# Holding the row scatters of an attention sequence until the twelfth exp of the next one

## The chip, the cores and the metric

The kernel runs on one core of one Trainium2 chip. The metric is the device time of one execution in microseconds (us). Three executions of the kernel before took 382.21, 382.22 and 384.64 us; the median is 382.22 us.

Engines are named as in the profile: PE (TensorE), with PEld for its weight loads, DVE (VectorE), ACT (ScalarE), POOL (GpSimd) and SP (SyncE, which here only issues DMAs).

## The reference

Attention with a learned bias over 8 sequences of 576 tokens and 8 heads of 64, and after it a mixture of 8 experts in which each token goes to the one expert that its domain id names.

```python
scores = (q @ k.T) / 8                               # per batch and head, 576 x 576
x = log1p(abs(i - j)) / log1p(max(i, 1))             # the same for all sequences
bias = relu(x[..., None] @ w1 + b1) @ w2             # hidden width 32, one value per head
attn = softmax(scores + bias)
rows = (attn @ v)                                    # back to 4608 rows of 512
for e in range(8):                                   # 1024 hidden
    mask = domain_id == e
    out[mask] = relu(rows[mask] @ moe_w1[e]) @ moe_w2[e]
```

## The kernel before

**Three stages.** First the bias tables are made, exp of the bias for all heads, kept in fast memory, and beside them the routing: for each token, the row of a scratch tensor `fire_x` in device memory to which it will go, so that the rows of an expert lie together (`posi`). Then attention runs over the sequences 0 to 7. Its results are scattered into `fire_x`, row by row, by indirect DMAs. Then the experts read `fire_x` back, transposed (`xT`, and `xA` for the first 512 rows of expert 0), multiply twice, and scatter the results into the output.

**Units of a sequence.** Each sequence has 21 units, numbered 0 to 20. A unit is a block of scores: PE multiplies (`scores`, lines 562 to 621), ACT takes the exp (line 614) of 128 x 1024 values, DVE multiplies by the bias table (`weight`, line 625). The order is: unit 0 `r0`, units 1 to 8 the main blocks of head pairs 0 and 1, unit 9 `r1`, units 10 to 13 head pair 2, units 14 and 15 `l0` and `l1` (last queries), unit 16 `x` (a quarter of the size, with a score buffer `scx` that it shares with the transposes), units 17 to 20 head pair 3. The scores of the others have two buffers, `sc`. The twelfth exp of a sequence is that of unit 11.

**The plan.** Behind each unit a written list, `PLAN`, says what else is done there. `T` and `D` transpose q and k of the next sequence on PE and copy them out on DVE; `V` copies v (`make_vext`); `W` weights a block; `A` multiplies by v into the accumulator `pu`, of which there is one (`av`, lines 630 to 658); `N` normalizes the result into a tile of rows (`norm`, lines 660 to 691). A mark ' says that it belongs to the sequence before. So the last four query blocks of head pair 3 of sequence b are finished at unit 7 of sequence b+1 (`N3'`), and its last 64 queries at unit 4 (`N4'`).

**Rows and scatters.** The rows of a sequence lie in two tiles: `xt` for 512 queries (four scatters of 128 rows of 1028 bytes, line 702) and `xl` for the last 64 (one scatter). Each has two buffers; a new one begins at `N0` (unit 11), where an iota on POOL writes the token numbers into its last columns (line 696). Half of `xl` is moved to its place by a copy that SP issues (line 691). In `norm`, as soon as head pair 3 is done, the four scatters of `xt` are issued, then a tiny memset of a tile `mark`, and then the scatter of `xl`. For sequence 7 the last norm is in two halves, each with its own two scatters.

**What sets the order.** PE, DVE and ACT execute in the order in which the code is written. POOL's queue is ordered by `_Issue` (lines 97 to 120): each DMA that POOL issues is kept behind the one that was written before it. The scatters of one group are free among each other, and whatever comes next stands behind all of them; this is what the memset of `mark` is for. Through POOL go, in a sequence b: the loads of q, k and their last rows for sequence b+2 (unit 2, lines 501 to 515), the scatters of sequence b-1 (unit 7), the load of v for b+2 with its last rows `vrag` (unit 8), the iotas (unit 11), and a load of a part of the experts' weights `w` (unit 12, line 983). In sequence 6 three more weight parts are loaded at unit 8 and one at unit 17. In sequence 7, SP issues the transposing read of `xA` at unit 9 (line 990). It has to wait for all scatters of sequences 0 to 6.

**Into the experts.** The first matmul of the experts (line 853) reads `xA`. The rest of expert 0 (line 861) reads `xT`, which waits for the scatters of sequence 7.

Of the kernel before, what the change touches and what calls it, by code (L numbers as in the profile page):

```python
# [13 lines left out]
AF = mybir.ActivationFunctionType  # L14
# [6 lines left out]
B = 8  # L21
# [71 lines left out]
def _ins(inst):  # L93
    return inst.ins if hasattr(inst, "ins") else inst
# [366 lines left out]
class _Attention:  # L461
# [100 lines left out]
    def scores(self, b, u):  # L562
        nc, G = self.nc, self.G
        mm = nc.tensor.matmul
        if u[0] == "x":
            sc = G.tps.tile([P, 1, 256], F32, tag="tr", name="scx", bufs=2)
        else:
            sc = G.aps.tile([P, 2, 512], F32, tag="sc", name="sc", bufs=2)

        j = self.joined.get(u)  # L570
        if j is None:
            e = self.new_e()
        else:
            if j == 0:
                self.e2 = self.new_e2()
            e = self.e2[:, 2 * j: 2 * j + 2, :]
        self.e[b, u] = e
        hs = (slice(0, 64), slice(64, 128))
        n = 1024
        if u[0] == "m":  # L580
            _, p, c = u
            raw = 2 * p >= RAW.get(c, H)
            if raw:
                for h2 in range(2):
                    mm(out=sc[:, h2, :], lhsT=G.idn, rhs=G.biasW[c][:, 2 * p + h2 - RAW[c], :],
                       start=True, stop=False)
            for h2 in range(2):
                mm(out=sc[:, h2, :], lhsT=self.qkT[b, p][hs[h2], 1, 128 * c: 128 * c + 128],  # L588
                   rhs=self.qkT[b, p][hs[h2], 0, :], start=not raw, stop=True)
            c0 = c if j is None else c - 1  # L590
            bias = None if raw else G.biasM[:, c0: c + 1, 2 * p: 2 * p + 2, :].rearrange("p c h i -> p c (h i)")
        elif u[0] == "r":
            for p in range(2):
                mm(out=sc[:, p, :], lhsT=self.qkTl[b][:, 2 * u[1] + p, 1, :],
                   rhs=self.qkT[b, 2 * u[1] + p][:, 0, :], start=True, stop=True)
            bias = G.biasR[:, 2 * u[1]: 2 * u[1] + 2, :].rearrange("p q i -> p (q i)")
        elif u[0] == "l":
            for lj in range(2):
                c = 2 * u[1] + lj
                for p in range(4):  # L600
                    mm(out=sc[:, lj, :].rearrange("k (h p q) -> k h p q", h=2, p=4)[:, :, p, :],
                       lhsT=self.qkT[b, p][:, 1, 128 * c: 128 * c + 128],
                       rhs=self.qkTl[b][:, p, 0, :].rearrange("k (h q) -> k h q", h=2),
                       start=True, stop=True)
            bias = G.biasL.rearrange("p u l h q i -> p (u l h q i)")
        else:
            n = 256
            for p in range(4):
                for h2 in range(2):
                    mm(out=sc[:, 0, 64 * p: 64 * p + 64], lhsT=self.qkTl[b][:, p, 1, :],  # L610
                       rhs=self.qkTl[b][:, p, 0, 64 * h2: 64 * h2 + 64], start=h2 == 0, stop=h2 == 1)
            bias = G.biasRL.rearrange("p q i -> p (q i)")
        ef, sf = e.rearrange("p a i -> p (a i)"), sc.rearrange("p a i -> p (a i)")
        nc.scalar.activation(out=ef[:, 0:n], in_=sf[:, 0:n], func=AF.Exp, bias=0.0, scale=0.125)  # L614
        if bias is None or j == 0:
            return None
        if j == 1:
            ef = self.e2.rearrange("p (c a) i -> p c (a i)", c=2) if u[0] == "m" else \
                self.e2.rearrange("p a i -> p (a i)")
            return ef, bias  # L620
        return (ef[:, 0:n].unsqueeze(1) if u[0] == "m" else ef[:, 0:n]), bias
# [38 lines left out]
    def norm(self, b, p, halves=(0, 1)):  # L660
        nc, asb = self.nc, self.G.asb
        pv = self.pu[:, :, 0:260].rearrange("p a (g d) -> p a g d", d=65)
        if p < 4:
            rz = asb.tile([P, 2, 4, 1], F32, tag="rz", name="rz", bufs=2)
            if p == 0:
                self.xt[b] = self.new_rows("xt", P, 4, S * b, 4)
                self.xl[b] = self.new_rows("xl", P, 1, S * b + 512, 1)
            a0, n = halves[0], len(halves)
            a = slice(a0, a0 + n)
            nc.vector.reciprocal(out=rz[:, a], in_=pv[:, a, :, 64:65])  # L670
            nc.vector.tensor_tensor(  # L671
                out=self.xt[b][:, 2 * a0: 2 * a0 + 2 * n, 128 * p: 128 * p + 128]
                .rearrange("p (a c) (g d) -> p a c g d", a=n, d=64),
                in0=pv[:, a, :, 0:64].rearrange("p a (c g) d -> p a c g d", g=2),
                in1=rz[:, a].rearrange("p a (c g) d -> p a c g d", g=2).to_broadcast([P, n, 2, 2, 64]),
                op=AO.mult)
            if p == 3:
                for t in range(2 * a0, 2 * a0 + 2 * n):
                    self.scatter(b, t, self.xt[b][:, t, :], 128)

                if b in self.xl:
                    self.G.issue(nc.gpsimd.memset(self.mark, 0.0))
                    self.scatter(b, 4, self.xl.pop(b)[0:64, 0, :], 64)
        else:
            rz = asb.tile([P, 2, 4, 1], F32, tag="rz", name="rz", bufs=2)
            xl = self.xl[b]
            pl = pv[:, 0]
            nc.vector.reciprocal(out=rz[:, 0], in_=pl[:, :, 64:65])
            nc.vector.tensor_tensor(out=xl[:, 0, 0:256].rearrange("p (g d) -> p g d", d=64), in0=pl[:, :, 0:64],
                                    in1=rz[:, 0].to_broadcast([P, 4, 64]), op=AO.mult)  # L690
            nc.sync.dma_start(out=xl[0:64, 0, 256:DM], in_=xl[64:128, 0, 0:256])

    def new_rows(self, tag, n, c, base, step):

        t = self.G.asb.tile([n, c, XW], F16, tag=tag, name=tag, bufs=2)
        self.G.issue(self.nc.gpsimd.iota(t[:, :, DM:].bitcast(I32), base=base, channel_multiplier=step,
                                         pattern=[[1, c], [0, 1]]))
        return t
# [19 lines left out]
    def run(self, late):  # L718
# [5 lines left out]
        for p in range(4):  # L724
            n = 4 if all(2 * p < RAW.get(c, H) for c in range(4)) else 2
# [23 lines left out]
        def plan(b, ui):  # L749

            if b < B - 1:
                return PLAN[ui].split()
            if b == B:
                return [w for w in PLAN[ui].split() if w[:2] not in ("A4", "N4")]
            return {19: "W16 N2 A40 A41", 20: "A42 A43 W18 N4"}.get(ui, PLAN[ui]).split()

        for n in range((B + 1) * NU):
            b, ui = divmod(n, NU)
            if b < B:
                jobs[b, ui] = self.scores(b, units[ui])  # L760
            if (b, ui) == (0, 5):
                self.nc.vector.memset(self.vx[1][:, :, :, 64:65], 1.0)
            if b == 0 and ui in (2, 6):
                self.transposes(0, 2 + ui // 6)
            if b == 0 and ui in (3, 7):
                self.take(0, 2 + ui // 7)
            if b < B - 2 and ui == 2:
                self.load_qk(b + 2)
                self.load_last(b + 2)
            if b < B - 2 and ui == 8:  # L770
                self.load_v(b + 2)
                self.load_vrag(b + 2)
            late(b, ui)
            for what in plan(b, ui):
                act(what.rstrip("'"), b - what.count("'"), n)
# [153 lines left out]
def kernel(  # L929
# [13 lines left out]
    nc = tc.nc  # L943
# [11 lines left out]
    with tc.manual_schedule(engines={ET.PE, ET.DVE, ET.Activation}):  # L955
        with ExitStack() as att:
# [20 lines left out]
            with tc.tile_pool(name="aps", bufs=1, space=PS, reuse_waits="tile") as G.aps:  # L977
                def late(b, ui):
                    if (b, ui) == (0, 2):
                        G.w.load(2, G.w_first)  # L980
                        _clear_overflow(tc, G, x_dram)
                    if 0 < b < 7 and ui == 12:
                        G.w.load(1, G.w_first)
                    if (b, ui) == (6, 8):
                        G.w.load(3, G.n4)
                    if (b, ui) == (6, 17):
                        G.w.load(1, G.n4)
                    if (b, ui) == (B - 1, 9):
                        G.early = G.n4("xA").rearrange("p (c t) -> p c t", c=4)
                        nc.sync.dma_start_transpose(out=G.early, in_=x_dram[0: EARLY, 0:DM])  # L990
                at.run(late)
# [36 lines left out]
```

## Time and profile before

| | us |
|---|---|
| median of three executions | 382.22 |
| the profiled execution | 384.64 |
| its span in the profile | 383.04 |
| PE busy | 330.2 (86%) |
| ACT busy | 250.6 (65%) |
| DVE busy | 237.0 (62%) |
| POOL busy | 180.4 (47%) |
| exps (line 614), busy and idle before them | 150.6 and 18.1 |
| scatters of `xt` (line 702), busy, mean of one | 40.2, 1.255 |
| attention's first exp of sequence 1, about | 88.8 |
| first matmul of the experts | 234.01 |

A time line of the profile gives the start in us from the start of the span, the length in us, the engine, the line of the kernel, the operation, what it writes and reads with the shapes, how many such instructions were merged into the row (x20), and in brackets the idle time of the engine just before the row and what ended it. The exps overlap a little: one takes 1.02 to 1.13 us, and the next starts about 0.90 us after it. The busy shares above are means over stages with different limits: in the stage of sequences 1 to 6 ACT and DVE are both busy nearly all the time, in the experts' stage PE alone is.

The ends of matmuls are modelled, and a small part of PE's records is missing in the trace.

### The profile page before, as it was taken

How to read it: one execution, taken by the hardware profiler on the slowest of the kernel's cores; microseconds unless marked ns; L12 is line 12 of the kernel's file. 1: busy time of each engine (PE TensorE's matmuls, PEld its weight loads, DVE VectorE, ACT ScalarE, POOL GpSimd, SP SyncE). 2: the span in 40 equal slices, each digit the busy share in tenths (PEclk: the TensorE clock that was granted, in tenths of full speed). 3: DMA queues.
4: the chain of work that ended last, by engine and by line, in shares of the span. 5: the costliest groups of instructions: out<-in, count | busy, mean ns of one | idle time of the engine just before them, and what ended most of it. 6: DMA issues, size and time to landing. Idle time of an engine off the chain costs nothing. (4 is left out here: it accounts for less than half of the span.)

```text
span 383.0 us, 9754 instructions
## 1 busy us (share of the span) xinstructions
PE 330.2 (86%) x4098; PEld 215.4 (56%) x4098; DVE 237.0 (62%) x450; ACT 250.6 (65%) x306; POOL 180.4 (47%) x236
## 2 busy tenths in 40 slices
PE   1488696959899898999898878999999999999990
PEld 0378673735657575656565554564646565565640
DVE  6999998739899999999999864212030302112130
ACT  8999996749799999999999963331505142332500
POOL 9260001883856859494546334234453635233241
PEclk9999999978999999999999989999999999999997
DMA  5999974939297999989727941699999999821221
GB/s 88 183 157 346 282 127 55 156 45 170 69 177 107 141 170 124 183 127 180 116 61 122 216 96 40 147 240 203 207 195 241 218 222 212 211 94 55 79 82 44
DMA packets 87668, 57.37 MB, mean 150 GB/s; under 512 B 44741, under 2 KB 78789, under 8 KB 87624
## 3 DMA queue, kind: packets, MB, share of 16 engines
q0 software_dynamic: 56960, 45.13, 69.5%
q1 hardware_dynamic: 30664, 11.62, 15.1%
q8 instruction: 32, 0.52, 0.6%
q14 instruction: 12, 0.10, 0.1%
HBM read 61.93 MB, written 24.70 MB: 226 GB/s over the span
## 5 line engine op out<-in xcount | busy, mean ns | idle before, releaser
L614 ACT ACTIVATE e<-sc 128x1024 f16<-128x1024 f32 x160 | 150.6, 1058 | 18.1 <-PE sc L588 11.0
L822 DVE COPY res<-ops 128x512 f32<-128x512 f32 x40 | 27.7, 692 | 109.4 <-PE ops L819 105.5
L879 ACT ACTIVATE hT<-hps 128x640 f16<-128x640 f32 x56 | 39.4, 704 | 78.1 <-PE hps L843 67.6
L625 DVE TENSOR_TENSOR e<-e,biasM 128x2048 f16<-128x2048 f16 x64 | 73.1, 1154 | 4.4 <-ACT e L614 4.1
L823 POOL DMA_INDIRECT out_dram<-res,ids x40 | 39.5, 987 | 74.2 <-DVE res L822 65.9
L819 PE MATMUL ops<-w,hT 128*128 128x512 f16 x320 | 70.7, 379 | 0.0
L702 POOL DMA_INDIRECT fire_x<-xt,posi x32 | 40.2, 1255 | 61.1 <-issue 45.6
L588 PE MATMUL sc<-qkT 64*128 64x512 f16 x256 | 53.1, 404 | 10.9 <-ACT e L614 7.9
L843 PE MATMUL hps<-xT,w 128*128 128x320 f16 x448 | 62.0, 299 | 0.0
L843 PEld LDWEIGHTS <-w 128*128 128x128 f16 x448 | 43.8, 98 | 18.1
L642 PE MATMUL pu<-vext,e 128*128 128x65 f16 x1024 | 51.6, 198 | 0.8 <-issue 0.4
L819 PEld LDWEIGHTS <-hT 128*128 128x128 f16 x320 | 31.2, 98 | 36.7 <-ACT hT L855 0.5
L642 PEld LDWEIGHTS <-e 128*128 128x128 f16 x1024 | 45.6, 101 | 3.1 <-issue 1.9
L787 POOL DMA_DIRECT2D w<-in_moe_w_dram x32 | 25.2, 792 | 18.7 <-DMA w<-in_moe_w_dram 7.1
L240 PE MATMUL eb<-W2BIG,e 128*128 128x32 f16 x432 | 19.6, 194 | 16.0 <-DVE e L223 9.6
L638 PE MATMUL pu<-vrag,e 128*128 128x130 f16 x128 | 29.6, 231 | 2.6 <-DVE xt L671 1.3
L588 PEld LDWEIGHTS <-qkT 64*128 64x128 f16 x256 | 16.6, 94 | 26.8 <-issue 17.3
L223 DVE TENSOR_SCALAR e<-L,slope,nb 128x576 f16<-128x576 f16 x86 | 31.1, 433 | 0.0
L240 PEld LDWEIGHTS <-e 128*128 128x128 f16 x432 | 17.5, 117 | 18.1 <-DVE e L223 10.9
L560 DVE COPY qkT<-pt 128x1024 f16<-128x1024 f16 x32 | 21.9, 685 | 5.3 <-PE sc L588 4.7
L671 DVE TENSOR_TENSOR xt<-pu,rz 128x512 f16<-128x512 f32 (+1 forms) x33 | 22.3, 675 | 1.8 <-DMA fire_x<-xt,posi 0.4
L638 PEld LDWEIGHTS <-e 128*128 128x128 f16 x128 | 12.7, 100 | 17.9 <-issue 11.3
(145 smaller groups left out, 394.0 us busy)
## 6 DMA issues: line engine op xcount, KB each, us to landing
w<-in_moe_w_dram POOLq DMA_DIRECT2D x32, 512.0 KB
fire_x<-zero SPq DMA_DIRECT2D x1, 5140.0 KB
qn<-in_q_dram POOLq DMA_DIRECT2D x8, 512.0 KB
kn<-in_k_dram POOLq DMA_DIRECT2D x8, 512.0 KB
vst<-in_v_dram POOLq DMA_DIRECT2D x8, 512.0 KB
out_dram<-res,ids POOLq DMA_INDIRECT x40
last<-zero SPq DMA_DIRECT2D x2, 256.0 KB
last<-in_q_dram POOLq DMA_DIRECT2D x16, 32.0 KB
```

The source lines that it names most:

```text
L223: nc.vector.tensor_scalar(out=hr, in0=G.L4[:, c0: c0 + S], scalar1=G.slope[:, m: m + 1], scalar2=G.nb1[:], op0=AO.mult, op1=AO.max)
L240: nc.tensor.matmul(out=eb[:, lj, 32 * k16: 32 * k16 + 32], lhsT=hr[:, jc: jc + 4 * 127 + 1: 4], rhs=G.W2BIG[:, 0:32], start=True, stop=True)
L588: mm(out=sc[:, h2, :], lhsT=self.qkT[b, p][hs[h2], 1, 128 * c: 128 * c + 128], rhs=self.qkT[b, p][hs[h2], 0, :], start=not raw, stop=True)
L614: nc.scalar.activation(out=ef[:, 0:n], in_=sf[:, 0:n], func=AF.Exp, bias=0.0, scale=0.125)
L625: self.nc.vector.tensor_tensor(out=job[0], in0=job[0], in1=job[1], op=AO.mult)
L638: mm(out=self.pu[:, c // 2, o: o + 130], lhsT=er[:, p % 2, 128 * c: 128 * c + 128], rhs=vr[:, p, :], start=True, stop=False, skip_group_ch ...
L642: mm(out=self.pu[:, c // 2, o + 65 * h2: o + 65 * h2 + 65], lhsT=self.e[b, ("m", p, j)][:, h2, 128 * c: 128 * c + 128], rhs=vx[:, 2 * p + ...
L702: inst = self.nc.gpsimd.indirect_dma_start(out=self.x_dram[:, :], out_offset=bass.IndirectOffsetOnAxis(ap=self.G.posi[0:n, c:c + 1], axis= ...
L819: nc.tensor.matmul(out=ops_, lhsT=hT[:, fc, t0: t0 + 128], rhs=G.w.w2(e, fc), start=(fc == 0), stop=(fc == 7))
L823: inst = nc.gpsimd.indirect_dma_start(out=out[:], out_offset=bass.IndirectOffsetOnAxis(ap=idx.bitcast(I32), axis=0), in_=res[:], in_offset ...
L843: nc.tensor.matmul(out=hps[:, i, 0:HC], lhsT=G.w.w1(e, dc)[:, 128 * fc: 128 * fc + 128], rhs=xT[:, dc, HC * hf: HC * hf + HC], start=(dc = ...
L879: nc.scalar.activation(out=hT[:, fc, :].rearrange("p (a b) -> p a b", a=2), in_=first(e, xT, ((fc, 0), (fc, 1))), func=AF.Relu, bias=0.0, ...
```

## The change

The scatters leave `norm`. `norm` now only notes that sequence b is ready (`self.ready`), but for the halves of sequence 7, which are scattered at once as before. The run loop issues the scatters of the ready sequence at unit 11 of the next one, and each of the four scatters of `xt` is made to wait for the exp of that unit. The memset of `mark` and the scatter of `xl` follow as before. The load of v and `vrag` moves from unit 8 to 12, the weight loads from 12 to 13 and (three in sequence 6) from 8 to 12, and the read of `xA` in sequence 7 from unit 9 to 12.

```diff
-        nc.scalar.activation(out=ef[:, 0:n], in_=sf[:, 0:n], func=AF.Exp, bias=0.0, scale=0.125)
+        self.exp = _ins(nc.scalar.activation(out=ef[:, 0:n], in_=sf[:, 0:n], func=AF.Exp, bias=0.0, scale=0.125))
...
             if p == 3:
-                for t in range(2 * a0, 2 * a0 + 2 * n):
-                    self.scatter(b, t, self.xt[b][:, t, :], 128)
-
-                if b in self.xl:
-                    self.G.issue(nc.gpsimd.memset(self.mark, 0.0))
-                    self.scatter(b, 4, self.xl.pop(b)[0:64, 0, :], 64)
+                if n == 1:
+                    self.scatters(b, (2 * a0, 2 * a0 + 1))
+                else:
+                    self.ready = b
...
+    def scatters(self, b, ts, behind=None):
+        for t in ts:
+            inst = self.scatter(b, t, self.xt[b][:, t, :], 128)
+            if behind is not None:
+                self.tc.add_manual_dep(_ins(inst), behind.name, mybir.DependencyInfo(
+                    mybir.DependencyClass.Sync, mybir.DependencyReason.DATA), reason="behind an exp")
+
+        if b in self.xl:
+            self.G.issue(self.nc.gpsimd.memset(self.mark, 0.0))
+            self.scatter(b, 4, self.xl.pop(b)[0:64, 0, :], 64)
...
                 jobs[b, ui] = self.scores(b, units[ui])
+            if 0 < b < B and ui == 11:
+
+                self.scatters(self.ready, range(4), self.exp)
...
-            if b < B - 2 and ui == 8:
+            if b < B - 2 and ui == 12:
                 self.load_v(b + 2)
                 self.load_vrag(b + 2)
...
-                    if 0 < b < 7 and ui == 12:
+                    if 0 < b < 7 and ui == 13:
                         G.w.load(1, G.w_first)
-                    if (b, ui) == (6, 8):
+                    if (b, ui) == (6, 12):
                         G.w.load(3, G.n4)
...
-                    if (b, ui) == (B - 1, 9):
+                    if (b, ui) == (B - 1, 12):
                         G.early = G.n4("xA").rearrange("p (c t) -> p c t", c=4)
                         nc.sync.dma_start_transpose(out=G.early, in_=x_dram[0: EARLY, 0:DM])
```

## The prediction

> **What bounds the kernel now.** I read the slices first, then the groups, then the timelines of ACT, GpSimd, DVE and PE around the scatters. From 88 to 231 us ACT runs the exps (line 614) almost without a break; from 234 to 362 us PE is at 90% or more and ACT waits for it. So an attention change moves the time only through ACT's breaks there, or through the moment at which the experts' first matmul (line 853) can start. The timeline of ACT, cut to the exps, shows every break of sequences 1 to 7:
>
> ```profile
> 101.75 1.02 ACT L614 ACTIVATE e<-sc 128x1024 f16<-128x1024 f32 x1 [0.92 <-PE sc L588]
> 104.02 1.94 ACT L614 ACTIVATE e<-sc 128x1024 f16<-128x1024 f32 x2 [1.25 <-PE sc L601]
> ...
> 125.62 0.38 ACT L614 ACTIVATE e<-scx 128x256 f16<-128x256 f32 x1 [0.56 <-PE sc L588]
> ...
> 145.39 0.38 ACT L614 ACTIVATE e<-scx 128x256 f16<-128x256 f32 x1 [0.58 <-PE sc L588]
> ...
> 165.16 15.88 ACT L614 ACTIVATE e<-sc 128x1024 f16<-128x1024 f32 x17 [0.32 <-PE sc L588]
> 181.27 2.86 ACT L614 ACTIVATE e<-sc 128x1024 f16<-128x1024 f32 x3 [0.22 <-PE sc L588]
> 184.62 0.38 ACT L614 ACTIVATE e<-scx 128x256 f16<-128x256 f32 x1 [0.50 <-PE sc L588]
> 204.27 0.38 ACT L614 ACTIVATE e<-scx 128x256 f16<-128x256 f32 x1 [0.56 <-PE sc L588]
> ...
> 222.82 1.94 ACT L614 ACTIVATE e<-sc 128x1024 f16<-128x1024 f32 x2 [1.27 <-DVE e L625]
> ```
>
> The last number of a row is the break before it. Sequence 1 loses 0.92 + 1.25 = 2.17 us, sequences 2 to 6 lose 0.56, 0.58, 0.32, 0.72 and 0.56, together 2.74. The sum over 1 to 6 is 4.91 us. Every one of them lies while GpSimd issues the scatters of the sequence before, or within 1 us after. The timeline of GpSimd for sequence 3:
>
> ```profile
> 137.34 1.26 POOL L702 DMA_INDIRECT fire_x<-xt,posi  x1 [4.70 <-DVE xt L671]
> ...
> 142.21 1.43 POOL L702 DMA_INDIRECT fire_x<-xt,posi  x1 [0.30 <-issue]
> 143.64 0.12 POOL L682 MEMSET mark<- 128x1 f16 x1
> 143.94 0.90 POOL L702 DMA_INDIRECT fire_x<-xl,posi  x1 [0.19 <-issue]
> 144.84 0.98 POOL L520 DMA_DIRECT2D vst<-in_v_dram  x1
> ```
>
> Scatters fill 137.34 to 144.84, 7.50 us. Now the same moment on PE and DVE:
>
> ```profile
> 143.88 0.41 PE L610 MATMUL scx<-qkTl 128*128 128x64 f16 x8
> ```
> ```profile
> 145.30 0.69 DVE L560 COPY qkT<-pt 128x1024 f16<-128x1024 f16 x1 [0.48 <-PE sc L588]
> ```
>
> PE has issued the scores of unit 16 (scx) by 144.29, yet their exp starts at 145.39, and DVE, which wants the transposes issued at 143.31 to 143.95, starts at 145.30, both about 0.5 us after the last scatter was issued. Two engines got PE's results about 1.1 to 1.3 us late. I call this the **hold**. Whether scatters cause it, or the dense PE work of units 12 to 17 that lies there too, the trace can't separate, because both have the same phase in every sequence.
>
> **The change, part by part.** No instruction is added or removed. In the built order PE, ACT, DVE and SP have the same instructions and waits as before. GpSimd's differs in two things: the first scatter of sequences 0 to 6 also waits for ACT, and the two iotas of a sequence (0.21 us each) stand before its v loads instead of behind them; the late weight loads keep their order behind them. Iotas feed scatters a sequence later: nothing.
>
> *The shift.* Before, a scatter starts 0.79 us after its rows are done: DVE's xt ends at 135.86 + 0.69 = 136.55, scatter at 137.34; for sequence 7 215.20 and 215.99. I take the same 0.79 behind an exp; the ends are 0 and 0.79, as the trace has no GpSimd wait for an exp here. Units 10 and 11 of sequence 3 end at 138.85 + 2.02 = 140.87, of sequence 7 at 217.50 + 2.02 = 219.52. So the scatters start at 141.66 and 220.31: **4.3 us later** (3.5 to 4.3), and end at 149.2 instead of 144.84, about unit 20 instead of unit 16.
>
> *What is queued behind the waiting scatter.* Four scatters, the mark, then v, vrag, w, q, k and last, all 4.3 us later. GpSimd idles 4.61 us before its next scatter (157.11); since all of its cycle shifts alike, that stays. The v loaded at 125.13 is copied by DVE at 149.82, 24.7 us later; the last rows of q and k issued from 130.03 to 132.64 are transposed at 150.01, 17 us later. The transfers are done by then: DMA share is 1.30 to 1.54 from 146.5 to 161, then 0.29, and sequence 5, which needs them, starts near 169. Cover after the shift: some 4 us, cost 0; beyond that each us is ACT's. The xt buffer that a norm writes was read by scatters one sequence ago; with 4.3 less of some 20 us left, 0.
>
> *The breaks.* The hold follows either the scatters or the units. If the scatters, it moves to units 17 to 20, where PE also has bursts (four A20 to A23 at unit 18) and the scores have the same two buffers of lead. If the units, nothing moves. Bounds for sequences 1 to 6: all 4.91 us gone, or every sequence pays what sequence 1 pays, 6 × 2.17 = 13.02, 8.1 more. I take the nearest rows, sequences 2 to 6, which pay the same 0.3 to 0.7 whatever they wait for, and let a fifth go, since the scores of unit 16 have a buffer of their own, and the moved scatters end close to the cheap start of the next sequence: **-1.0 us**.
>
> [...] The 145.30 and 145.39 rows above speak for the scatters, without proof.
>
> *The end of attention.* Sequence 7 loses 1.27 us in the hold, and then, in a table of stretches (length, busy time of PE, weight loads, DVE, ACT and GpSimd with their instructions, then granted clock, DMA share, GB/s):
>
> ```profile
> 221.30:224.70 3.40, 1.50 (x22) 0.98 (x19) 2.12 (x3) 2.13 (x4) 2.34 (x5) 1.00 0.21 63
> 224.70:228.10 3.40, 3.29 (x40) 2.42 (x39) 1.73 (x4) 2.17 (x4) 0.00 (x0) 0.50 0.53 94
> ```
>
> PE is busy 1.50 of 3.40 us, and in the next window its granted clock is 0.50; ACT then waits 1.44 and 0.83 us for it. So 1.27 + 1.44 + 0.83 = 3.54 us are lost. But the experts start here:
>
> ```profile
> 225.08 2.23 SPq L990 DMA_TRANSPOSE xA<-fire_x  x1
> ```
> ```profile
> 234.01 7.07 PE L853 MATMUL hps<-xA,w 128*128 128x512 f16 x32
> ```
>
> xA reads what all scatters up to sequence 6 wrote: it goes 9.09 us after the first of them (215.99), and the DMA share falls to 0.00 at 229.0. With the shift it goes at 229.4 and lands at 233.3. Line 853 starts at 234.01 now, with no wait for xA: slack 5.0 us now, **0.7 us** afterwards. So of 3.54 us at most 0.7 can be won, as xA is late next. The hold and half clock can also come 4.3 us later, over the last av matmuls; I take **-0.5 us** (bounds: -0.7, and +2.3, the cold stretch on the last norms as on the exps now). On SP the last xl copy (231.33) stands behind xA, which holds the queue to 229.4 + 2.23 = 231.6: 0.3 us late, under the 1.3 us between its landing (4.0 median, 235.3) and its scatter at 236.67. Its cost is 0.
>
> **The sum.** -1.0 - 0.5 = -1.5 us. The profiled execution took 384.64 us (span 383.04), so 383.1; it lies 2.42 above the median of the three, 382.22, so **380.7 us**.
>
> **Rivals.** Faster: the hold needs both scatters and dense units, and the shift parts them. For it: units 0 to 11 run without a break of this kind. Against: units 18 to 20 are dense too. Price -4.91 - 0.7 = -5.6: **376.6 us**, or 378 if a quarter stays. Slower: the hold falls on the scores of units 19, 20 and 0, which ACT needs at once, where no separate buffer covers them; for it, sequence 1, which pays 2.17. It decides from 0.82 + 3.8 / 6 = 1.45 us per sequence; at 2.17 in half of the sequences and the present price in the others it gives +4.1, **386.3 us**, at 2.17 in all 390.3. Slower at one place: xA lands later than 9.09 + 3.8 us behind the first scatter, for instance because the weight loads that moved with the scatters are in its way; each us past 0.7 is one us of the end, and 3.4 us at half clock cost the first matmuls 1.7: **383 to 385 us**. That the hold does nothing is excluded by the 4.3 us; that time doesn't feel it (the hold belongs to the units) gives **382.2**.
>
> **Chances.** Forecast and its neighbours (hold moves along, or time doesn't feel it, 379 to 384): 0.56. Faster rival: 0.24. Slower, by the hold or by xA: 0.20. One per cent, 3.8 us, is about what a measurement of this kernel can tell from no change. Eight in ten: 376.8 (nearly all breaks gone) to 386.3 (the hold at its higher price in half of the sequences).
>
> **What would show it.** Scatters starting 3.5 to 4.3 us later against the exps, always behind the twelfth; breaks of ACT near units 17 to 20 and 0 (forecast), none (faster) or over 1.45 us per sequence (slower); breaks still at scx (units); xA issued near 229 and line 853 without idle before it. I am wrong if GpSimd's scatters get much shorter or longer in the new place, or if a load comes late.

## The result and the profile after

The changed kernel took 406.64 us (406.63, 406.64 and 408.07), the kernel before 382.22 us (382.21, 382.22, 384.64) on the same chip: 1.063 times the time, with a 95% interval from 1.056 to 1.070. The prediction was 380.7 us with a range up to 386.3: the time lies 20 us above its upper end. The profiled execution took 406.63 us, its span is 405.09 us (before 383.04) and its mean granted clock 0.925 (before 0.98).

The timeline of ACT of the changed kernel, cut to the exps; these rows answer to the same view shown of before:

```profile
148.90 0.38 ACT L614 ACTIVATE e<-scx 128x256 f16<-128x256 f32 x1 [0.65 <-PE sc L588]
149.18 1.93 ACT L614 ACTIVATE e<-sc 128x1024 f16<-128x1024 f32 x2
153.57 1.94 ACT L614 ACTIVATE e<-sc 128x1024 f16<-128x1024 f32 x2 [2.46 <-PE sc L588]
155.69 1.02 ACT L614 ACTIVATE e<-sc 128x1024 f16<-128x1024 f32 x1 [0.18 <-PE sc L594]
156.93 1.02 ACT L614 ACTIVATE e<-sc 128x1024 f16<-128x1024 f32 x1 [0.21 <-PE sc L588]
158.44 1.02 ACT L614 ACTIVATE e<-sc 128x1024 f16<-128x1024 f32 x1 [0.48 <-PE sc L588]
159.67 12.13 ACT L614 ACTIVATE e<-sc 128x1024 f16<-128x1024 f32 x13 [0.21 <-PE sc L588]
...
177.11 1.94 ACT L614 ACTIVATE e<-sc 128x1024 f16<-128x1024 f32 x2 [2.70 <-remote]
```

The break at scx (unit 16) is still there, 0.65 us, and a new one of 2.46 us stands before unit 19 (153.57). The next sequence begins at 155.69, and its first units have breaks too. The same pattern is in every sequence from 1 to 6; before unit 19 they lose 2.00, 2.43, 2.46, 2.70, 2.46 and 2.48 us.

GpSimd at the end of sequence 4 (timeline):

```profile
168.92 1.93 POOL L711 DMA_INDIRECT fire_x<-xt,posi  x1 [8.85 <-DVE qkT L560]
171.16 0.99 POOL L711 DMA_INDIRECT fire_x<-xt,posi  x1 [0.31 <-issue]
172.46 0.96 POOL L711 DMA_INDIRECT fire_x<-xt,posi  x1 [0.30 <-issue]
173.73 0.96 POOL L711 DMA_INDIRECT fire_x<-xt,posi  x1 [0.30 <-issue]
174.69 0.12 POOL L699 MEMSET mark<- 128x1 f16 x1
175.00 0.90 POOL L711 DMA_INDIRECT fire_x<-xl,posi  x1 [0.19 <-issue]
```

And PE, then DVE, in the same microseconds (timelines):

```profile
173.13 0.22 PE L638 MATMUL pu<-vrag,e 128*128 128x130 f16 x1
173.18 0.42 PE L642 MATMUL pu<-vext,e 128*128 128x65 f16 x8
173.92 0.41 PE L588 MATMUL sc<-qkT 64*128 64x512 f16 x2 [0.32 <-issue]
174.46 0.59 PE L585 MATMUL sc<-biasW,idn 128*128 128x512 f16 x2
174.98 0.39 PE L588 MATMUL sc<-qkT 64*128 64x512 f16 x2
178.19 1.01 PE L594 MATMUL sc<-qkT,qkTl 128*128 128x512 f16 x2 [2.81 <-ACT e L614]
```
```profile
177.07 0.21 DVE L670 RECIPROCAL rz<-pu 128x8 f32<-128x8 f32 x1 [3.01 <-remote]
```

PE has issued the last av of the unit by 173.60 and the scores of units 19 and 20 by 175.37. DVE, which waits for the av result, starts at 177.07, ACT on the scores of unit 19, issued by 174.33, at 177.11. Both are released together, 3.5 and 2.8 us after PE's part by the profile, and 1.2 us after the last scatter was issued (175.90). Whether the results are late or only the signals that tell of them, the profile doesn't show. This is the hold of the prediction, and it has grown: before, it was 1.1 to 1.3 us. Now ACT stops, PE has nothing to do for 2.81 us because it needs a free score buffer, and the table of stretches (length, busy time of PE, weight loads, DVE, ACT and GpSimd, then granted clock, DMA share, GB/s) shows what follows:

```profile
170.09:173.50 3.41, 3.41 (x72) 2.63 (x71) 3.38 (x5) 3.05 (x5) 2.72 (x3) 1.00 0.24 80
173.50:176.91 3.41, 1.42 (x10) 0.57 (x7) 0.56 (x2) 0.91 (x1) 2.98 (x6) 1.00 0.32 99
176.91:180.32 3.41, 2.13 (x24) 0.83 (x23) 3.22 (x5) 2.96 (x3) 3.41 (x6) 0.50 0.79 92
180.32:183.74 3.42, 3.42 (x47) 2.25 (x46) 2.47 (x6) 2.57 (x3) 2.60 (x5) 0.50 1.38 171
```

PE is busy 1.42 of 3.41 us, and in the next 6.83 us its granted clock is 0.50: the first units of the next sequence pay for that (a pair of score matmuls takes 0.61 us at 179.82, 0.39 at 174.98).

At the other end, the first matmul of the experts now waits for `xA` (PE's timeline; 234.01 before, without a wait):

```profile
253.66 9.60 PE L865 MATMUL hps<-xA,w 128*128 128x512 f16 x32 [0.88 <-DMA xA<-fire_x]
```

**Where the 22.05 us of the span came from.** Up to the first exp of sequence 1: -0.99 (88.82, now 87.83). Sequences 1 to 6: 119.59, now 138.92, +19.33. From the first exp of sequence 7 to the first expert matmul: 25.60, now 26.91, +1.31. From there to the end: 149.03, now 151.43, +2.40; the block of 32 matmuls at line 865 alone takes 9.60 us in place of 7.07, since until 258.83 the granted clock is 0.50 (before, 1.00 over the whole block).

Some single executions, of the kernel before too, take 8 to 53 us longer, which those that were profiled lose in the experts' stage; they are left out of the times below, and of such a profile only the attention is read.

### The profile page after: what moved, and what is told of

Its sections match the earlier page's. It is cut to its first block, busy times and chain, and to the rows that moved or that the text cites. A ratio compares the mean times of both kernels' runs of the same rounds, so it can differ in the third digit from the quotient of the medians.

```text
span 405.1 us, 9761 instructions
## 1 busy us (share of the span) xinstructions
PE 343.6 (85%) x4098; PEld 219.4 (54%) x4098; DVE 237.1 (59%) x450; ACT 252.5 (62%) x306; POOL 179.4 (44%) x236
## 5 line engine op out<-in xcount | busy, mean ns | idle before, releaser
L614 ACT ACTIVATE e<-sc 128x1024 f16<-128x1024 f32 x160 | 152.2, 1044 | 29.9 <-PE sc L588 23.1
L834 DVE COPY res<-ops 128x512 f32<-128x512 f32 x40 | 27.7, 692 | 112.9 <-PE ops L831 112.9
L711 POOL DMA_INDIRECT fire_x<-xt,posi x32 | 38.5, 1204 | 82.0 <-DVE qkT L560 55.5
L588 PE MATMUL sc<-qkT 64*128 64x512 f16 x256 | 56.5, 436 | 3.6 <-ACT e L614 2.3
L642 PE MATMUL pu<-vext,e 128*128 128x65 f16 x1024 | 53.2, 199 | 3.9 <-issue 3.7
L588 PEld LDWEIGHTS <-qkT 64*128 64x128 f16 x256 | 14.2, 95 | 21.8 <-issue 14.4
L594 PE MATMUL sc<-qkT,qkTl 128*128 128x512 f16 x32 | 12.9, 496 | 15.2 <-ACT e L614 15.2
```

The lines of the kernel that those rows point to most:

```text
L614: self.exp = _ins(nc.scalar.activation(out=ef[:, 0:n], in_=sf[:, 0:n], func=AF.Exp, bias=0.0, scale=0.125))
L642: mm(out=self.pu[:, c // 2, o + 65 * h2: o + 65 * h2 + 65], lhsT=self.e[b, ("m", p, j)][:, h2, 128 * c: 128 * c + 128], rhs=vx[:, 2 * p + ...
L711: inst = self.nc.gpsimd.indirect_dma_start(out=self.x_dram[:, :], out_offset=bass.IndirectOffsetOnAxis(ap=self.G.posi[0:n, c:c + 1], axis= ...
```

## The experiments

The kernel before ran beside every group of experiments. On one chip it took 383.8 to 386.9 us, about as in the first measurement; on the five other chips 367 to 370 us. I call the first kind **late chips**, the second **prompt chips**. That difference turned out to matter more than anything else, and it came up in the first group. (Whether it belongs to the chip itself or to something else that stayed the same during a group isn't known; no chip showed both.)

Theory A: the scatters cause the hold, and the shift puts it where ACT, DVE and PE have no cover. Rivals: the hold belongs to the units; or the moved loads and `xA` are what costs.

### Without the scatters, first on a prompt chip

The kernel before, without the scatters of sequences 0 to 6:

```diff
-            if p == 3:
+            if p == 3 and b == B - 1:
```

> The kernel before, with the scatters of sequences 0 to 6 left out (their rows never reach the experts; the last sequence's scatters stay). Theory A, the hold goes with the scatters: the breaks of ACT in units 12 to 17 (4.9 us in sequences 1 to 6) go, and the half clock at the end of attention with them; 373 to 378 us. Theory B, the hold belongs to the dense PE units: the breaks stay at scx, about 382 us.

365.2 us (364.2 to 365.7), 0.990 times before [0.985, 0.995]. The sequences take 18.81 us each, without a break. But before itself took 368 us here, so only 3 us were there to win: on this chip there is no hold to take away. The run says nothing on its cause.

### The loads moved alone

The kernel before with the moves of v, w and `xA` (units 12, 13, 12), the scatters where they were.

> The kernel before with the moved loads of the change alone (v at unit 12, weights at 13 and 12, xA at 12); the scatters stay at unit 7 with no wait for an exp. Theory A: same as before within 2 us (380 to 384). Theory C, the late loads make the change slow: 395 us or more.

Its two executions took 412.1 and 400.2 us. The profiled one, of 412.1, takes 193.4 us from the first expert matmul to the end, where the run without scatters on this chip takes 147.1, so these times can't be compared. The attention can be read: sequences of 18.80 to 18.84 us with all their scatters, 20 exps in a row without a break. The moved loads cost nothing in the attention, and the scatters nothing on this chip.

### The hold alone, and a hold until unit 17

The changed kernel with the loads put back to units 8, 12 and 8; and the changed kernel with `ui == 17` in place of `ui == 11` and `xA` at unit 18.

> The change with v and weights at their old units (8, 12, 8), so that only the scatters are held. Theory A: as slow as the change, 400 to 409 us, with the breaks of ACT of 2 to 2.7 us before unit 19 and half clock in each sequence. Theory C: about 382 us.

> The change with the scatters held to the exp of unit 17 in place of 11, so that they run from unit 18 to unit 4 of the next sequence (v and weights then stand ahead of them). Theory A1, the price is made by the place, the 36 matmuls of unit 18 beside the later scatters: the break before unit 19 shrinks below 1 us, 383 to 392 us. Theory A2, scatters cost some 3 us per sequence wherever they run behind unit 12: 400 us or more, with the break at units 0 to 4.

375.4 us (374.7 and 376.1; 1.020 [1.010, 1.029]) and 375.6 us (375.4 and 375.8; 1.020 [1.014, 1.027]), both on the same prompt chip, so neither tells of the hold. Nor does the first hold its scatters where the changed kernel does: the v loads stand in front of them and are issued late, and the scatters of sequences 0 to 4 start 5.5 to 10.7 us behind the twelfth exp, not 0.79. It is the only one of the two with breaks in the attention, and these are of another kind. PE's timeline and two rows of ACT's:

```profile
159.43 1.10 PE L535 MATMUL ptl<-idn,last 128*128 128x128 f16 x8 [2.05 <-DMA last<-in_q_dram]
```
```profile
161.11 1.02 ACT L614 ACTIVATE e<-sc 128x1024 f16<-128x1024 f32 x1 [2.36 <-PE sc L588]
...
182.30 4.69 ACT L614 ACTIVATE e<-sc 128x1024 f16<-128x1024 f32 x5 [1.57 <-PE sc L588]
```

With the v loads in front of the held scatters, the loads of q, k and the last rows came too late in sequences 5 and 6: 2.36 + 1.57 = 3.9 us (at the end its first expert matmul also waits 1.83 us for `xA`). The hold until unit 17 has sequences of 18.8 to 18.9 us and loses at the end instead; the experts' first matmul:

```profile
223.78 9.22 PE L865 MATMUL hps<-xA,w 128*128 128x512 f16 x32 [6.01 <-DMA xA<-fire_x]
```

It waits 6.01 us for `xA`, and its block takes 2.15 us more than 7.07, at half clock (0.50 granted from 217.93 to 224.75): 8.2 us in the trace, 7 in the time. So `xA` has the price that the prediction gave it, one us per us and some 2 us for the clock.

### The changed kernel again, beside one without scatters and one held until unit 14

One group, which fell on a late chip: the changed kernel unaltered, the kernel before without scatters once more, and the changed kernel held to unit 14:

```diff
-            if 0 < b < B and ui == 11:
+            if 0 < b < B and ui == 14:
...
-                    if (b, ui) == (B - 1, 12):
+                    if (b, ui) == (B - 1, 15):
```

> The changed kernel once more, unaltered. On the chip of the first four experiments no late PE result (hold) was seen, and the kernel before took 368 us there instead of 382. Theory A (the +24 us are the hold, which the shift moves from units 12 to 16 to units 18 to 20, where ACT and PE then stand still and PE's clock falls to half): where the hold exists (before near 382 us) 405 to 408 us, with ACT breaks of 2.0 to 2.7 us before unit 19 of every sequence; where it does not exist (before near 368 us) no such breaks, sequences of 18.8 to 19.0 us, and only the late xA is paid, 0 to 4 us more than before. Rival (the later loads and the later xA cost the 24 us by themselves, whatever the state of the chip): 20 to 26 us more than before on any chip.

> The kernel before without the scatters of sequences 0 to 6 (fire_x keeps no rows of them), the same as in the first call. Theory A: where the hold exists, the breaks of ACT in sequences 1 to 6 (4.9 us) and the 7.5 us by which sequence 1 begins later than on the other chip go with the scatters: 10 to 14 us less than before; where it does not exist 2 to 4 us less. Rival (the hold belongs to the units, or to the chip's memory as a whole): the breaks stay, within 3 us of before, on any chip.

> The changed kernel with the scatters held until unit 14 instead of 11, and xA read behind unit 15. Theory A: where the hold exists it falls 3 units later, on the end of unit 20 and units 0 and 1 of the next sequence; PE has the transposes of the next sequence done by then, and its scores have two buffers of lead, so breaks of 1.5 to 3 us at units 0 to 2, 400 to 410 us; where it does not exist no breaks, and xA later by 3 units, which makes 3 to 6 us more than before. Rival (the 24 us are the later loads and xA): 2 to 3 us more than the changed kernel on any chip.

Before took 383.8 to 386.9 us here. The changed kernel: 408.0 and 411.5 us, breaks of 2.0 to 2.5 us before unit 19 again, sequences of 22.2 to 23.9 us. Without scatters: 370.9 us (368.9 to 371.3), 0.961 times before [0.952, 0.969]. The latter's timeline of ACT:

```profile
158.00 0.45 ACT L614 ACTIVATE e<-scx 128x256 f16<-128x256 f32 x1
158.28 18.71 ACT L614 ACTIVATE e<-sc 128x1024 f16<-128x1024 f32 x20
```

20 exps in a row, 18.81 us per sequence, no break at scx or anywhere in sequences 1 to 6. The units, PE's dense stretches and the loads are all still there: on a late chip the hold is there with the scatters and gone without them. The rival "the hold belongs to the units" falls.

That the chip was late during this very execution shows in sequence 0. There the kernel fills `fire_x` with zeros by eight other indirect scatters (line 433), which this run keeps (GpSimd's timeline, first and last of them; then ACT's):

```profile
71.83 1.08 POOL L433 DMA_INDIRECT fire_x<-zero,pi  x1 [0.30 <-issue]
...
82.42 1.62 POOL L433 DMA_INDIRECT fire_x<-zero,pi  x1 [0.30 <-issue]
```
```profile
74.70 1.02 ACT L614 ACTIVATE e<-sc 128x1024 f16<-128x1024 f32 x1 [0.83 <-PE sc L588]
77.71 1.02 ACT L614 ACTIVATE e<-sc 128x1024 f16<-128x1024 f32 x1 [1.99 <-PE pu L642]
80.00 1.94 ACT L614 ACTIVATE e<-sc 128x1024 f16<-128x1024 f32 x2 [1.27 <-DVE e L625]
```

The same kernel on the prompt chip has the same eight scatters, from 71.84 to 84.10, and no such break beside them:

```profile
68.80 7.68 ACT L614 ACTIVATE e<-sc 128x1024 f16<-128x1024 f32 x8 [0.35 <-PE sc L588]
76.30 0.46 ACT L614 ACTIVATE e<-scx 128x256 f16<-128x256 f32 x1
76.58 18.73 ACT L614 ACTIVATE e<-sc 128x1024 f16<-128x1024 f32 x20
```

Sequence 0 takes 30.39 us here, 28.0 to 32.4 in the five profiles of late chips, and 23.8 to 25.0 in all those of prompt ones. So one part of the expectation was wrong: the late start of sequence 1 did not go with the scatters taken out (first exp at 86.98; 88.82 before, 80.52 in the run on the prompt chip). No run left out the scatters of line 433, so that they cause it is not shown.

Held until unit 14: 382.4 to 386.3 us, 0.998 times before [0.993, 1.002]. I expected 400 to 410. The same scatters, three units later, cost over 20 us less than at unit 11. In the attention (ACT's timeline):

```profile
178.73 0.41 ACT L614 ACTIVATE e<-scx 128x256 f16<-128x256 f32 x1
179.00 6.76 ACT L614 ACTIVATE e<-sc 128x1024 f16<-128x1024 f32 x7
186.27 12.22 ACT L614 ACTIVATE e<-sc 128x1024 f16<-128x1024 f32 x13 [0.51 <-PE sc L588]
```

One break of 0.48 to 0.59 us per sequence, before unit 3 of the next one, and sequences of 19.6 to 19.9 us. Only in sequence 7, which has no next sequence to prepare, does the hold of this kernel fall on units 17 to 20, and there it is as dear as in the changed kernel: ACT loses 3.48 and 0.82 us before units 19 and 20. DVE and PE:

```profile
222.01 0.21 DVE L670 RECIPROCAL rz<-pu 128x8 f32<-128x8 f32 x1 [2.54 <-remote]
```
```profile
223.00 0.26 PE L653 MATMUL pu<-vrag,e 128*64 128x65 f16 x2 [3.00 <-DVE rz L670]
```

The stretches of this one kernel show both kinds, first around a hold before unit 3, then around that of sequence 7:

```profile
181.40:184.80 3.40, 3.22 (x58) 1.80 (x57) 3.40 (x5) 3.40 (x5) 2.79 (x3) 1.00 0.40 126
184.80:188.20 3.40, 2.54 (x46) 1.66 (x45) 2.68 (x6) 2.89 (x5) 1.70 (x5) 1.00 0.23 68
188.20:191.60 3.40, 3.19 (x61) 2.13 (x59) 3.37 (x5) 3.40 (x5) 3.01 (x4) 1.00 0.43 66
...
218.70:222.10 3.40, 1.30 (x31) 0.95 (x27) 0.86 (x3) 1.28 (x2) 2.48 (x4) 1.00 0.30 99
222.10:225.50 3.40, 2.50 (x36) 1.16 (x37) 1.94 (x3) 1.21 (x2) 2.56 (x3) 0.50 0.21 70
```

With PE busy 2.54 of 3.40 us the clock stays at 1.00; with 1.30 it falls to 0.50. So the price of a hold has two parts in these runs: what ACT can't cover with its two score buffers (0.51 us in the first place, 3.48 and 0.82 in the second), and, behind the stretch in which PE was busy 1.30 of 3.40 us, the half clock.

### The changed kernel on a prompt chip

> The changed kernel, unaltered. On a chip where PE's results come late beside the scatters (before near 383 us) it takes 406 to 412 us as twice so far; on a chip where they don't (before near 368 us) Theory A expects no break before unit 19, sequences of 18.8 to 19.1 us and only the later xA: 368 to 373 us, that is 0 to 5 us more than before. The rival (moved loads and xA are dear by themselves) expects 20 us more than before on either.

372.0 us (371.1 to 372.6), 1.011 times before [1.008, 1.013], which took 368.5 us. The attention has no break (ACT's timeline), and the end has one (PE's):

```profile
133.17 18.72 ACT L614 ACTIVATE e<-sc 128x1024 f16<-128x1024 f32 x20
151.76 0.41 ACT L614 ACTIVATE e<-scx 128x256 f16<-128x256 f32 x1
```
```profile
218.98 8.85 PE L865 MATMUL hps<-xA,w 128*128 128x512 f16 x32 [1.92 <-DMA xA<-fire_x]
```

A wait of 1.92 us, and 8.85 in place of 7.07 us for the block: 3.7 us, where the time shows 3.6. That the block is longer by half clock is an estimate: the two groups of eight av matmuls just ahead of it take 0.65 and 0.64 us in place of 0.42, as they do at the granted 0.50 in the profile of the changed kernel on the late chip (230.61). (7.07 is the block at a granted clock of 1.00, as in the kernel before; in runs of prompt chips that don't wait for `xA` it takes 7.07 to 8.42.) Everything that the change moves besides the hold costs this much on a prompt chip: about 3.6 of the 24 us. The remaining some 20 us need a late chip, and there they are not the loads either: in both profiles of the changed kernel on late chips PE, DVE and ACT have no wait for a load in sequences 1 to 6, but for 0.2 us in all. The rival "moved loads and `xA` cost the 24 us" falls.

### Trying to pay neither

Two kernels were to avoid the hold at units 17 to 20. In one, the four scatters of sequences 0 to 5 stand apart, and those of sequence 6 go at once, with all loads and `xA` as before:

```diff
+            if 0 < b < B - 1 and ui in (9, 11, 13, 15):
+                self.scatters(self.ready, ((ui - 9) // 2,), self.exp)
```

In the other they are held until unit 14, those of sequence 6 again at once, and `xA` is read behind unit 9.

The scatters of the first do not stand as the edit says. The v loads of unit 8 are in front of them in GpSimd's order and are issued late, so in all its profiles those of sequences 0 to 4 start between unit 18 and unit 6 of the next sequence, with the iotas and a weight load between the second and the third; only those of sequence 5 come near their units (12, 13, 17 and 18).

> The kernel before, with the four scatters of sequences 0 to 5 apart: each waits for an exp of its own, those of units 9, 11, 13 and 15 of the next sequence, and xl behind the last. Sequence 6 is scattered at once, loads and xA stand where they stood before. Theory A (PE's results are held as long as GpSimd issues scatters back to back; a single one of 1.0 to 1.9 us is covered by the two score buffers, 1.8 us of exps): the breaks at units 12 to 16 of sequences 2 to 6 (4.9 us in all) go but for some 0.3 us each, sequences of 18.9 to 19.3 us instead of 19.7: 377 to 380 us where before takes 382 to 384. Rival (each scatter holds PE by itself, wherever it falls): four holds instead of two per sequence, breaks of 0.6 us at four places, 387 to 392 us.

> The scatters of sequences 0 to 5 held until unit 14 as in the experiment before, but those of sequence 6 at once, and xA read behind unit 9 as in the kernel before. Theory A (a hold is dear on units 17 to 20, cheap elsewhere; in the run with unit 14 the sequences took 19.6 us, and sequence 7 lost 3.7 and 0.9 us before units 18 and 19): sequence 7 is again as in the kernel before, 379 to 381 us where before takes 382 to 384. Rival (what is dear belongs to sequence 7 whatever is scattered there): 382 to 384 us as before.

Both fell on prompt chips. Apart: 366.4 and 368.6 us, and on another prompt chip 368.0 us (366.5 to 370.5; 1.000 [0.997, 1.003]).

Unit 14 and sequence 6 at once: 367.5 us (366.3 to 369.1; 0.999 [0.996, 1.001]). Neither beats the kernel before where there is no hold to avoid. Whether they do on a late chip is open, and what a single scatter costs there as well.

### A direct DMA in the place of the scatter

To tell the indirect form from the bytes and the queue, the changed kernel with

```diff
-        inst = self.nc.gpsimd.indirect_dma_start(
-            out=self.x_dram[:, :],
-            out_offset=bass.IndirectOffsetOnAxis(ap=self.G.posi[0:n, c:c + 1], axis=0),
-            in_=x, in_offset=None)
+        inst = self.nc.gpsimd.dma_start(out=self.x_dram[128 * c: 128 * c + n, :], in_=x)
```

The rows are not sorted by expert. Since `xA` then depends on sequence 0 alone, it is also read earlier, and its wait goes too.

> The changed kernel with a direct DMA of the same rows, bytes and queue in the place of each indirect scatter; the rows go to fire_x in the order of the tokens, so that the experts multiply as many rows, but not their own. Tells whether the hold belongs to the indirect form. Theory A1 (GpSimd's work for 128 single row addresses holds PE's results): no breaks before unit 19, sequences of 18.8 to 19.1 us, 370 to 376 us, most of the rest being the later xA. Theory A2 (the bytes written or the DMA as such hold them): breaks of 2 to 2.7 us as in the changed kernel, 400 to 408 us.

368.4 us (366.5 to 368.7; 0.999 [0.997, 1.002]) and, on another chip, 367.2 us: prompt chips both times. This kernel and the one with the scatters apart also ran with plain reads of `fire_x` in the place of the transposed ones, the direct one three times and the other twice, the first time with an expectation for the sequences alone, then with these:

> The changed kernel with direct DMAs of the same rows and bytes in the place of the indirect scatters, and with plain reads of the same bytes of fire_x in the place of the transposing ones (the experts multiply numbers that are not theirs, as many as before). Where the kernel before takes 382 to 384 us: 368 to 374 us, and sequences 1 to 6 of 18.8 to 19.1 us without a break before unit 19, if the indirect form makes PE's results late; 400 to 408 us, sequences of 22 to 24 us with breaks of 2.0 to 2.7 us, if the bytes or the queue do. Where the kernel before takes 368 us: 366 to 369 us again, which tells nothing.

> The kernel before with the scatters of sequences 0 to 5 apart, behind the exps of units 9, 11, 13 and 15, and with plain reads of the same bytes of fire_x in the place of the transposing ones (the experts multiply numbers that are not theirs). Where the kernel before takes 382 to 384 us: 372 to 378 us and sequences of 18.8 to 19.4 us if a single scatter is covered by the two score buffers; 385 to 392 us, over 20 us each, if every scatter makes PE's results late at a price of its own. Where the kernel before takes 368 us: 366 to 369 us again.

Direct: 368.3 us (1.000 [0.998, 1.003]), 368.1 us and 367.6 us (0.996 [0.994, 0.999]). Apart: 367.4 us, and 367.9 us (0.997 [0.995, 0.999]). Before took 367 to 370 us beside them: prompt chips, and no answer. What in a scatter makes PE's results late is not settled.

## Why the prediction was wrong

**The step that failed** is the term "The breaks", taken as -1.0 us with the words that the nearest rows, sequences 2 to 6, "pay the same 0.3 to 0.7 whatever they wait for". Measured, sequences 1 to 6 pay +19.33 us; the breaks alone, as the prediction counted them, grow from 4.9 to about 23 us. Against the 112.84 us of six sequences without scatters on a late chip, the kernel before pays 119.59 - 112.84 = 6.8 us, the changed one 26.1. By the starts of the exps these 26.1 are some 14 us before unit 19, 5 at scx, and 7.5 in unit 20 and the first units of the next sequence, at half clock (0.50 from 176.91 to 183.74 in the table above).

The hold did move along with the scatters, as the forecast had it. ACT's main break ends 7.9 to 8.1 us after the first scatter of the group in sequences 2 to 6 of the kernel before (unit 16 or 17), 8.1 to 8.2 in sequences 1 to 6 of the changed one (unit 19), and 7.5 to 7.6 with the hold until unit 14 (unit 3 of the next sequence). What changed is which results are due at that moment. It is not enough that scatters run beside a unit: those held until unit 14 run beside units 17 to 20 as well (178.75 to 186.43 in sequence 4, whose exps are shown above), without a break there.

The row I priced it by was paid under cover; so I read the rows, as no run changed the buffers. At units 12 to 16 the late results are scores that lie one or two units ahead of ACT, and transposes whose reader can wait. At units 17 to 20 they are the last av into the single `pu`, which DVE needs for the norm that PE's next av waits for, and the scores of the last two units; ACT runs out, frees no buffer, and so PE runs out as well. I wrote down that the new place has "the same two buffers of lead", which is 1.8 us of exps, and took the hold of 1.1 to 1.3 us along as it was, without a reason. It isn't fixed: up to 3.5 us in the new place. Why it lasts longer there is open. The run held until unit 14 agrees on the place: the same scatters cost 0.8 to 1.1 us per sequence there. The break at scx, which the prediction named as a sign for the units, is no such sign: in the changed kernel it ends 3.5 us after the first held scatter, so unit 16 lies beside the scatters in both kernels.

**The slower rival** had the mechanism, the scores of units 19, 20 and 0 without cover, and the point from which it decides, 1.45 us per sequence. Its price was too small: 2.17 us was the dearest row of the trace, and it was taken for the end of the range. The measured price is 26.1 / 6 = 4.3 us. No row of before shows what a hold costs where all three engines come to a stop, and the trace did hold a warning that I used only for the end: the half clock behind sequence 7's hold (PE busy 1.50 of 3.40, then 0.50). I priced it once, and it came with every sequence.

**The shift** was right: the twelfth exp's end and the first scatter are 0.79 us apart in all seven sequences, the value that I took. **What is queued behind** was right: the moved loads cost nothing in the attention (18.8 us per sequence with them on prompt chips, no wait for them on late ones). The case with the loads put back shows that this order was not free to choose: 3.9 us.

**The end** was right in mechanism and wrong in sum. I said that `xA` is late next, that its slack falls from 5.0 to 0.7 us, and that each us past it costs one, with 1.7 for the half clock. In the result `xA` went 9.07 us after the first scatter (I had 9.09), but 22.60 after the first exp of sequence 7 (I had 21.0), because the first units there ran at half clock too (0.50 from 224.70 to 234.94): +1.31 to the first expert matmul and +2.40 behind it. On a prompt chip it went 20.96 us after that exp, as I had it; but there the experts are ready after 23.5 us instead of 25.6, and the slack is gone: 1.92 us of wait and 1.78 of a longer block. Both ways -0.5 should have been +3.7, by the price that the rival "xA lands later" gave: one us per us, and the half clock.

**Scatters or units.** The prediction could not separate the two; its rows at 145.30 and 145.39 spoke for the scatters. On a late chip the breaks go when the scatters go (0.961 times before, 18.81 us per sequence), so the units alone can't be the cause. How a scatter makes PE's results late is not shown.

## What to carry to other kernels

Before moving work that disturbs another engine, don't carry its price along from the old place: ask at the new place how many microseconds each reader of the disturbed results can wait, which buffers are single, and whether the disturbed engine itself runs dry, since here the half clock came on top (0.50 granted behind stretches with PE busy 1.30 to 1.50 of 3.4 us). The hold that cost breaks of 0.3 to 0.7 us in sequences 2 to 6 where the late scores lay ahead of ACT cost them 2.4 to 2.7 us before unit 19. And when a cost shows in a trace without a cause (here the hold), measure the kernel without the suspect before building on it; repeat that on more than one chip.

## What was not expected of the hardware

- The same kernel takes 367 to 370 us on five chips and 382 to 387 in two measurements elsewhere. By the attention's profiles about half of the 14 us lies in sequence 0 (32.4 against 23.8 to 25.0 us) and half in sequences 1 to 6 (119.6 against 112.9, 18.8 each). The change costs 1.1% on the one kind and 6.3% on the other.
- On late chips, PE's results reach ACT and DVE up to 3.5 us late beside indirect scatters, two at once (177.07 and 177.11 above), and at times DVE and ACT read in the profile as waiting for "remote". On prompt chips the same scatters at the same units don't do it (20 exps in a row in 18.72 us).
- Half clock was granted from 176.91, when PE had been idle for 1.54 us (since 175.37; the whole gap was 2.81), behind a stretch in which it was busy 1.42 of 3.41 us, and not behind one with 2.54 of 3.40.
